# Two small loads moved in the weight queue of a recurrent loop, and eight more weight blocks loaded ahead of it

## The chip, the cores and the metric

The kernel runs on one core of a Trainium2 chip. The metric is device time in microseconds (us). Every run named here was put in the fast state by its own time, but for one repeat of one experiment, which is left out. Single executions of one kernel scatter by some 0.5%, and a profiled execution is one of the timed ones. So sizes are taken from the timed ratios, and traces are used to say where the time lies. The record marks every run as correct. One of them (e14) was made wrong on purpose, and the check passed it all the same, so the check does not guard what that run broke.

## The reference, cut to what matters

Two heads are computed and concatenated. Head B, a state-space convolution, comes first in the kernel and concerns us only in that the weights of head A are preloaded during its last phase. Head A is the loop:

```python
for s in range(n_seg):                                # 64 segments of 32 rows
    xs = x[:, s * seg_len:(s + 1) * seg_len, :].copy()
    h = jnp.concatenate([mem, xs], axis=1)            # 8 memory rows + 32 rows
    q, k, v = (jnp.einsum('btd,dhe->bhte', h, W) for W in (Wq, Wk, Wv))   # 32 heads of 128
    scores = jnp.einsum('bhqe,bhke->bhqk', q, k) * scale      # then mask, softmax p
    o = jnp.einsum('bhqk,bhke->bhqe', p, v)
    o = jnp.einsum('bhte,hed->btd', o, Wo)
    mem = o[:, :M, :].copy()                          # the next segment needs this one
    outs.append(o[:, M:, :])
```

(The three projections are written as one line here.) The steps can't overlap much, since each needs the memory rows of the one before. The kernel keeps only a part of the four weights (32 MB) on the core and loads the rest again in every step.

## The kernel before

A step uses 64 weight blocks of 512 KB. Most are resident, two are kept packed in PSUM, and 17 are streamed in each step through a ring of five slots. All streamed blocks are issued by the sync engine, in program order, so one queue carries the weights and the small loads and stores between them. `between` hangs a small load ahead of a streamed block. The loop's matmuls work on the 8 memory rows and 24 of a segment's 32 rows (the "x columns"); keys, queries and values of the other 8 rows (the "left rows") were computed before the loop and are loaded. A block's slot is free when the last matmul on the block five loads earlier has ended.

```python
STREAM = {("k", 0): (0, 5), ("q", 0): (1, 5), ("k", 1): (0, 3), ("q", 1): (0, 4), ("v", 0): (0, 4), ("v", 1): (0, 4)}
STREAM_O = (0, 4, 8, 11, 13)
SLOTS = 5
EARLY = 26                                            # resident blocks loaded before the loop

def unit(key):                                        # cut: resident and kept blocks return at once
    between.pop(key, lambda: None)()                  # a small load first, on the same queue
    t_ = wst.tile([128, 2048], BF16, name="wst", tag="w%d" % (loads[0] % SLOTS))
    loads[0] += 1
    nc.sync.dma_start(out=t_[:], in_=WD[key][:])
    return t_

def load_pk(j):                                       # "left rows": 128 x 768, 192 KB
    pk = pers.tile([128, 768], BF16, name="pk", tag="pk")     # one buffer
    nc.sync.dma_start(out=pk[:], in_=PKd[j])
    return pk

def load_xt(j):                                       # "x columns": 128 x 192, 48 KB
    xt = work.tile([128, KC, XM], BF16, name="xt", tag="F")   # shares its buffer with lb0b
    nc.sync.dma_start(out=xt[:].rearrange("p k r -> p (k r)"), in_=XTd[j])
    return xt

for s in range(NS):
    between["k", 0, 5] = lambda: pks.append(load_pk(s))
    if s:
        between["k", 1, 3] = lambda: stores(s - 1, ob)
    a = quads("k", 0, range(KC))                      # key projection, half 0
    pk = pks[0]
    k0 = evac(a, "A")
    KT0 = new_kt(0)                                   # copies left keys out of pk
    a = quads("q", 0, range(KC))
    # ... cut: k 1, q 1, scores, softmax, v 0, v 1; lb0b (tag "F") is written
    pv0 = pv_x(0, V0, pb0, [lb0a, lb0b])              # first value product: last reader of lb0b
    # ... cut
    oproj(pp[:, 1, :], range(0, 7), o0)
    # ... cut: second value product
    oproj(pp[:, 1, :], (7,), o0)
    pv_l(pl_, 1, V1, L1)                              # second left product: last reader of pk
    if s + 1 < NS:
        between["o", 11] = lambda: put_xt(load_xt(s + 1))
    oproj(pp[:, 1, :], range(8, 12), o1)
    fetch(("o", 15))                                  # unpacks a kept block
    oproj(pp[:, 1, :], range(12, 16), o1)
    # ... cut: output cast, memory rows into hT
```

## Time and profile before

2635.57 us median of 3 runs (2634.26 to 2643.28). The prediction shows the profile's lines; this table has the marks that the later sections use, in us from the start of the span of the profiled execution.

| mark | before |
|---|---|
| last matmul of head B's inverses ends | 868.0 |
| first x columns issued on the sync queue | 870.1 |
| first output cast of the loop (end of step 0) | 925.4 |
| last output cast | 2572.3 |
| end of span | 2634.1 |

63 steps lie between the two casts. What is to be read from the table is that the loop is 1647 of 2634 us, so a microsecond a step is 2.4% of the kernel.

### The profile page before, as it was taken

To read this page: it belongs to the slowest core of one execution; us is meant where nothing else is said; L and a number is where in the kernel's file an instruction comes from. 1 tells how busy PE (TensorE), PEld (TensorE's weight loads), DVE (VectorE), ACT (ScalarE), POOL (GpSimd) and SP (SyncE) were. 2 spreads that over 40 slices of the span, in tenths; PEclk is the share of its full clock that TensorE was granted. 3 is DMA by queue.
4 is the path that set the end of the run, shared out by engine and by line. 5 is a ranking of instruction groups with operands and counts; after the bars stand their busy time and mean duration, and the time that the engine had idled before them with its cause. 6 is when DMAs were issued, how large, how long until landed. Compare 5 with 4: busy or idle time off the path is not lost.

```text
span 2634.1 us, 76564 instructions
## 1 busy us (share of the span) xinstructions
PE 2085.4 (79%) x32902; PEld 1106.9 (42%) x32902; DVE 1496.4 (57%) x3224; ACT 1023.4 (39%) x1550; POOL 312.6 (12%) x601
## 2 busy tenths in 40 slices
PE   1588788776887688888888888888888787888788
PEld 1364555532333244444444444444444444444444
DVE  9677787879882245454545454454545454545450
ACT  6888888931222123232323323232323232322221
POOL 2233333450001100000000000000000000000010
PEclk6799999988898799899999999999999999999999
DMA  5665864742338999999999999999999999999992
GB/s 138 163 193 172 243 177 138 191 133 80 119 131 296 340 362 356 351 360 363 355 357 356 373 350 367 351 367 358 362 359 356 361 361 359 354 370 354 358 366 88
DMA packets 382386, 763.17 MB, mean 290 GB/s; under 512 B 118678, under 2 KB 210806, under 8 KB 379998
## 3 DMA queue, kind: packets, MB, share of 16 engines
q1 hardware_dynamic: 364158, 704.64, 76.1%
q0 software_dynamic: 14128, 39.99, 4.5%
q10 hardware_dynamic: 3760, 13.65, 1.4%
q8 instruction: 257, 4.21, 0.6%
q14 instruction: 83, 0.68, 0.1%
HBM read 703.35 MB, written 67.88 MB: 293 GB/s over the span
## 4 chain that ended last, share of the span: by engine, by line
DMA 35%; PE 30%; DVE 14%; ACT 9%; issue 8%; SPq 1%; POOL 1%; ACTq 0%; DVEq 0%; POOLq 0%
PE acc L329 15%; DMA wst<-WD_k 13%; DMA wst<-WD_o 13%; DMA wst<-WD_q 4%; DMA wst<-WD_v 2%; PE pp L428 2%; PE pe L551 2%; ACT sn L1019 2%; PE tr L340 2%; PE pro L151 2%; ACT kM L994 1%; ACT E L991 1%; ACT ev L335 1%; DVE piece L268 1%; PE ups L850 1%
## 5 line engine op out<-in xcount | busy, mean ns | idle before, releaser
L329 PEld LDWEIGHTS <-hT 128*32 128x32 bf16 x12352 | 334.8, 99 | 502.0 <-issue 293.2
L329 PE MATMUL acc<-wst,hT 128*32 128x512 bf16 x3072 | 321.7, 403 | 164.3 <-DMA wst<-WD_k 91.9
L335 ACT CAST ev<-acc 128x512 bf16<-128x512 f32 x384 | 225.1, 586 | 455.7 <-PE acc L329 451.4
L428 PEld LDWEIGHTS <-oT 128*32 128x32 bf16 x8192 | 205.6, 97 | 160.8 <-issue 134.5
L329 PE MATMUL acc<-W_q,hT 128*32 128x512 bf16 x3072 | 235.0, 391 | 0.0
L329 PE MATMUL acc<-W_k,hT 128*32 128x512 bf16 x2816 | 222.2, 417 | 0.0
L428 PE MATMUL pp<-W_o,oT 128*32 128x256 bf16 x5120 | 213.6, 277 | 6.6 <-DMA W_o<-in_A_Wo_dram 6.6
L329 PE MATMUL acc<-W_v,hT 128*32 128x512 bf16 x3072 | 213.5, 381 | 6.3 <-DMA W_v<-in_A_Wv_dram 6.3
L268 DVE TENSOR_SCALAR piece<-keep 128x256 int32<-128x256 int32 (+1 forms) x640 | 189.2, 362 | 48.3 <-PE pp L428 31.4
L341 DVE COPY KT<-tr 128x512 bf16<-128x512 bf16 x64 | 27.2, 425 | 304.7 <-PE tr L340 304.7
L367 DVE TENSOR_REDUCE mx<-sc 128x8 f32<-128x320 f32 x128 | 62.4, 488 | 236.6 <-PE sc L360 236.4
L428 PE MATMUL pp<-wst,oT 128*32 128x256 bf16 x2560 | 130.3, 280 | 78.5 <-DMA wst<-WD_o 69.3
L348 POOL COPY KT<-pk 128x128 bf16<-128x128 bf16 x128 | 37.9, 296 | 958.9 <-PE acc L329 545.2
L1158 PE MATMUL yp<-Bt,mi 128*128 128x512 bf16 x384 | 115.1, 408 | 40.5 <-DMA mi<-MId 31.8
L341 ACT COPY QT<-tr 128x512 bf16<-128x512 bf16 x128 | 75.0, 586 | 179.2 <-PE tr L340 178.3
L415 ACT CAST oT<-pv 128x512 bf16<-128x512 f32 x128 | 75.1, 586 | 173.4 <-PE pv L401 171.7
L995 DVE SCALAR_TENSOR_TENSOR nr<-kM,ptt 128x656 f32<-128x656 f32 x128 | 104.9, 833 | 43.7 <-ACT kM L994 43.4
L151 PE MATMUL pro<-xTl,wsl 128*128 128x512 bf16 x512 | 117.8, 384 | 11.6 <-DVE kst L155 7.4
L369 ACT ACTIVATE sc<-sc 128x320 f32<-128x320 f32 x128 | 54.0, 422 | 153.0 <-DVE sc L368 150.3
L518 ACT CAST ob<-pp 128x128 bf16<-128x128 f32 x64 | 17.0, 266 | 246.2 <-DVE ob L517 246.2
L1074 PE MATMUL hps<-KT,MF 128*128 128x512 bf16 x384 | 94.4, 395 | 19.4 <-DVE x L1087 15.2
L994 ACT ACTIVATE kM<-ptt,magic 128x656 f32<-128x656 f32 x128 | 104.2, 814 | 6.8 <-PE ptt L931 6.8
(285 smaller groups left out, 3661.3 us busy)
## 6 DMA issues: line engine op xcount, KB each, us to landing
wst<-WD_o SPq DMA_DIRECT2D x320, 512.0 KB
wst<-WD_k SPq DMA_DIRECT2D x256, 512.0 KB
wst<-WD_q SPq DMA_DIRECT2D x256, 512.0 KB
wst<-WD_v SPq DMA_DIRECT2D x256, 512.0 KB
Ud<-ux POOLq DMA_DIRECT2D x16, 1024.0 KB, 4.7
uq<-Ud SPq DMA_DIRECT2D x32, 512.0 KB
pk<-PKd SPq DMA_DIRECT2D x64, 192.0 KB
wsl<-in_A_Wk_dram SPq DMA_DIRECT2D x16, 512.0 KB
```

Of the source, the lines that this page charges most:

```text
L151: nc.tensor.matmul(a[:], lhsT=w[:, kc, 128 * j:128 * j + 128], rhs=xTl[:, kc, :, :].rearrange("p s k -> p (s k)"), start=(kc == 0), stop=( ...
L268: nc.vector.tensor_scalar(out=out.bitcast(I32), in0=in_.bitcast(I32), scalar1=0, scalar2=None, op0=ALU.bitwise_or)
L329: nc.tensor.matmul(a[32 * g:32 * g + 32, o_:o_ + rhs.shape[1]], lhsT=hT[:, kc, :], rhs=rhs, start=(kc == 0), stop=(kc == KC - 1), tile_pos ...
L335: nc.scalar.copy(out=q[:], in_=a[:])
L341: eng(out=dst, in_=p[:, i, :, :, :])
L367: nc.vector.tensor_reduce(out=mx[:], in_=sc, axis=AX.X, op=ALU.max)
L415: nc.scalar.copy(out=o[:], in_=p[:].rearrange("p a (g q) -> p a g q", g=4))
L428: nc.tensor.matmul(po[32 * qt:32 * qt + 32, :], lhsT=oT[:, h % 4, (h % 16) // 4, :], rhs=columns(w, 1024 * hh + 256 * qt, 256)[0][1], star ...
L994: sc.activation(out=kM[:], in_=ptv, func=ACT.Identity, bias=magic[:])
L995: v.scalar_tensor_tensor(out=nrs[e // 4][:, e % 4].rearrange("p f t j -> p f (t j)"), in0=kM[:], scalar=MAGIC, in1=ptv, op0=ALU.subtract, ...
L1074: pe.matmul(ps[:], lhsT=MF[:, 4 * rr + mc, cs, 128 * kc:128 * kc + 128], rhs=rhs, start=(i == 0 and mc == 0), stop=(i == 1 and mc == 3))
L1158: pe.matmul(yp[:], lhsT=m_[:, cs, kc, :], rhs=Bt[:, kc, half, j, c_, :], start=(n == 0), stop=(n == 15))
```

## The change

Its intent: each small load is to stand in the queue where it need not wait longer than the block behind it would wait anyway. The x columns go from ahead of output block 11 to ahead of 13, the left rows from ahead of key block (0,5) to ahead of query block (0,1). And eight more resident blocks are loaded during head B's last phase (10 into buffers that were free by then, 24 as before), so that fewer are left for the first step.

```diff
-EARLY = 26
+EARLY = 24
...
-        between["k", 0, 5] = lambda: pks.append(load_pk(s))
+        between["q", 0, 1] = lambda: pks.append(load_pk(s))
         if s:
             between["k", 1, 3] = lambda: stores(s - 1, ob)
         a = quads("k", 0, range(KC))
+        k0 = evac(a, "A")
+        a = quads("q", 0, range(KC))
         pk = pks[0]
...
-        k0 = evac(a, "A")
         KT0 = new_kt(0)
-        a = quads("q", 0, range(KC))
         q0 = evac(a, "B")
...
-            between["o", 11] = lambda: put_xt(load_xt(s + 1))
-        oproj(pp[:, 1, :], range(8, 12), o1)
+            between["o", 13] = lambda: put_xt(load_xt(s + 1))
+        oproj(pp[:, 1, :], range(8, 14), o1)
         fetch(("o", 15))
-        oproj(pp[:, 1, :], range(12, 16), o1)
+        oproj(pp[:, 1, :], range(14, 16), o1)
...
     def residents():
+        def put(t_):
+            load_resident(tc, None, src, rest.pop(0), W_res, tc.nc.scalar, t_)
+        four = ahead.pool.tile([128, 4, 2048], BF16, name="W4", tag="kst")
+        for i in range(4):
+            put(four[:, i, :])
+        yield
+        two = ahead.pool.tile([128, 2, 2048], BF16, name="W2", tag="xTl")
+        for i in range(2):
+            put(two[:, i, :])
+            yield
+        for _ in range(4):
+            put(ahead.pool.tile([128, 2048], BF16, name="W1", tag="wsl", bufs=4))
+            yield
```

Cut: the pools are opened earlier and closed later so that these buffers exist, and the first four blocks are issued at the start of the second pointwise half.

More of the change, by code (lines that the diff above doesn't have):

```diff
@@ L175, with load_resident @@
     pass
-EARLY = 26
-def load_resident(tc, pool, src, key, W_res, eng=None):
-    t_ = pool.tile([128, 2048], BF16, name="W_%s" % "_".join(str(i) for i in key))
+EARLY = 24
+def load_resident(tc, pool, src, key, W_res, eng=None, t_=None):
+    if t_ is None:
+        t_ = pool.tile([128, 2048], BF16, name="W_%s" % "_".join(str(i) for i in key))
     (eng or tc.nc.sync).dma_start(out=t_[:].rearrange("e (h d) -> e h d", h=2) if key[0] == "o" else t_[:], in_=src(key))
@@ L600, in part_b @@
     v.memset(magic[:], MAGIC)
+    ahead.open(ahead.ctx)
     ctx_m = ctx.enter_context(ExitStack())
@@ L603, in part_b @@
     MF = mfp.tile([128, 16, 2, 512], BF16, name="MF")
-    ctx_p = ctx.enter_context(ExitStack())
-    ahead.open(ctx_p)
     ctx1 = ctx.enter_context(ExitStack())
@@ L1042, in part_b @@
     ctx1.close()
-    bp = ctx.enter_context(tc.tile_pool(name="b_B", bufs=2))
+    bp = ctx.enter_context(tc.tile_pool(name="b_B", bufs=1))
     Dsk = const.tile([128, D], BF16, name="Dsk")
@@ L1051, in part_b @@
     ktp = ctx2.enter_context(tc.tile_pool(name="b_KT", bufs=1))
+    bp0 = ctx2.enter_context(tc.tile_pool(name="b_B0", bufs=1))
     pw = ctx2.enter_context(tc.tile_pool(name="b_pw", bufs=1))
@@ L1171, in part_b @@
     for dh in range(2):
-        Bt = bp.tile([128, 4, 2, 2, 2, DH], BF16, name="Bt", tag="B")
+        Bt = (bp0, bp)[dh].tile([128, 4, 2, 2, 2, DH], BF16, name="Bt", tag="B")
         Bs.append(Bt)
         if dh == 1:
+            resident = residents()
+            next(resident)
             todo = [(0, c) for c in range(16)] + [(1, c) for c in range(16)]
@@ L1183, in part_b @@
     ctx2.close()
-    ctx_p.close()
     ctx_m.close()
-    resident = residents()
     for c in range(16):
@@ L1224 @@
     rest = Keys(RESIDENT)
-    rest.ctx = ctx_w
+    rest.ctx = ahead.ctx = ctx_w
     def residents():
+        def put(t_):
[11 more added lines that the diff above has]
+            yield
         pool = ctx_w.enter_context(tc.tile_pool(name="a_wre0", bufs=1, side="right"))
```

## The prediction

> **What bounds the kernel now.** I read the page first, then busy time by stage, then the waits of the DMA queue and of TensorE, then one iteration of the loop on the queue.
>
> The page's slices show three regimes: preparation with DMA at 2 to 8 tenths, a loop from about 870 us with DMA at 9, a short tail. The chain that ended last is mostly DMA of streamed weight blocks (`wst`).
>
> ```profile
> PE   1588788776887688888888888888888787888788
> ...
> DMA  5665864742338999999999999999999999999992
> ...
> DMA 35%; PE 30%; DVE 14%; ACT 9%; issue 8%; SPq 1%; POOL 1%; ACTq 0%; DVEq 0%; POOLq 0%
> ```
>
> Busy time by stage (us of PE, PEld, DVE, ACT, POOL, then granted clock, DMA share, GB/s). I cut at the start of the inverse phase that preloads weights, at its end, at the first output cast of the loop (925.4) and at the last (2572.3).
>
> ```profile
> 798.00:860.00 62.00, 49.95 (x205) 20.70 (x204) 12.15 (x31) 15.33 (x23) 8.13 (x15) 0.92 0.96 335
> 860.00:872.00 12.00, 8.32 (x45) 3.52 (x42) 3.87 (x10) 2.94 (x5) 5.22 (x25) 1.00 0.39 131
> 872.00:925.40 53.40, 32.03 (x424) 13.28 (x424) 13.40 (x36) 8.39 (x14) 1.25 (x4) 0.63 1.02 389
> 925.40:2572.30 1646.90, 1360.28 (x26839) 702.65 (x26840) 816.88 (x2268) 487.06 (x945) 70.79 (x203) 0.96 0.98 359
> ```
>
> The loop's 63 later steps take 1646.9 / 63 = 26.14 us each, at DMA share 0.98 and 359 GB/s. PE is busy 83%. The first step takes 53 us because it also loads 19 resident blocks. Between 860 and 872 the DMA is mostly idle.
>
> Waits of the DMA queue in the loop, then of PE (us in total, times, longest):
>
> ```profile
> SPq L298 <- PE pv L401: 163.7, 62, 3.1
> SPq L293 <- PE pp L401: 137.1, 62, 2.9
> ```
>
> ```profile
> PE acc L329 <- DMA wst<-WD_k: 85.4, 105, 2.0
> PE pp L428 <- DMA wst<-WD_o: 66.6, 80, 2.8
> PE acc L329 <- DMA wst<-WD_q: 29.8, 90, 1.6
> ```
>
> L298 loads the next x columns, L293 the left rows. Each blocks the queue for a reason that has nothing to do with the weights: 2.6 and 2.2 us per step. PE waits for streamed blocks 85.4 + 66.6 + 29.8 + 4.8 (values) = 187 us in the loop, 3.0 us per step. One step on the queue (start, duration), and the DMA in 4 us stretches of it:
>
> ```profile
> 1719.28 2.95 SPq L246 DMA_DIRECT2D wst<-WD_o  x3
> 1724.91 0.32 SPq L298 DMA_DIRECT2D xt<-XTd  x1
> 1725.29 1.76 SPq L246 DMA_DIRECT2D wst<-WD_o  x2
> 1727.13 0.38 SPq L246 DMA_DIRECT2D wst<-WD_k  x1
> 1729.48 0.32 SPq L293 DMA_DIRECT2D pk<-PKd  x1
> 1729.85 0.42 SPq L246 DMA_DIRECT2D wst<-WD_k  x1
> ```
>
> ```profile
> 1718.00:1722.00 4.00, 4.00 (x90) 2.02 (x76) 2.90 (x7) 2.15 (x5) 0.30 (x1) 1.00 0.94 351
> 1722.00:1726.00 4.00, 3.81 (x88) 1.61 (x80) 3.65 (x11) 1.87 (x5) 0.00 (x0) 1.00 0.99 380
> 1726.00:1730.00 4.00, 3.50 (x92) 2.48 (x94) 3.31 (x10) 1.10 (x2) 0.35 (x1) 1.00 0.75 243
> ```
>
> No issue goes out between 1722.2 and 1724.9; the two output blocks then follow the x columns back to back, so their slots had been free. One DMA latency later the share falls to 0.75. The loop is DMA-bound, but its queue is fed with two holes.
>
> **What the Trainium skill says.** "Perfetto Trace Analysis", section "Sequencer Loop" and its DMA timeline under "Per-instruction lifecycle": a DMA's semaphore wait is served in the issuing sequencer, before the window shown. So a waiting small load holds everything behind it. The trace agrees (the 2.7 us hole above). "DMA: Bandwidth & Descriptors", section "Issuing engines are not separate DMA queues": DMAs of the scalar and sync engines run on the same 16 engines. It agrees: with both issuing in 798 to 860 the share is 0.96, no more. So preloading gains only where those engines idle. "Perfetto Trace Analysis", section "Roofline": 358 GB/s is the per-core share, about 435 GB/s the ceiling of the 16 engines when one core is active. The loop's 359 with 389 in its first step says that the loop isn't at the ceiling.
>
> **The change part by part.** The streamed blocks (17 of 512 KB a step), the five slots and the arithmetic stay. Comparing the instruction orders, PE, VectorE and GpSimd keep the order of their work; what moves is the queue of the sync engine and the preloads issued by ScalarE.
>
> (a) x columns ahead of output block 13. Their buffer is free once the first value product of the step has been read, which PE reaches just before value block (1,4). The slot of output block 11 is freed by value block (1,0), earlier; that of 13 by (1,4), later. So the old place blocks 11 and the new one blocks nothing. I paired each streamed load with the last matmul on the block five loads before. Block 11 is issued a median 1.63 us after its slot is free, 13 is 0.63 us late; unhindered ones are 0.03 to 0.05 us late.
>
> (b) Left rows ahead of query block 1. Their buffer is read until the second left product, after output block 7. The slot of key block 5 is freed by output block 4, before it, that of query block 1 by output block 8, after it. Key block 5 is a median 2.56 us late, query block 1 0.39 us.
>
> What these holes cost: I put the block packets of steps 3 to 60 in order of their start. From one block to the next takes 1.33 to 1.4 us where the queue is full (query to value blocks), 2.19 from output 11 to 13 and 2.36 from key 5 to query 1. The small loads take DMA time themselves, 0.20 us (x) and 0.66 us (left rows), from their packets' durations. Lost are 2.19 - 1.35 - 0.20 = 0.64 us and 2.36 - 1.35 - 0.66 = 0.35 us, together 1.0 us a step or 63 us in 63 steps. That is a ceiling for the removal of the holes. PE's waits at the blocks concerned average 0.17 (o11), 0.77 (o13), 0.55 (key 5) and 0.23 us (query 1), 1.7 us a step, so PE can take the gain. I count a bit over half, 0.55 us a step. The ring has only five slots, PE frees them unevenly, and blocks that now come early may find PE late. 63 x 0.55 = 35 us.
>
> (c) 34 blocks ahead instead of 26. Eight resident blocks leave the first step, which runs at 389 GB/s: 8 x 524,288 B / 389 GB/s = 10.8 us off it (the first step is DMA-bound at share 1.02). Where they go: four are issued at the start of the second pointwise half, near 645 us, where the DMA share is 0.2 to 0.3: free, 4 x 1.4 = 5.6 us into at least 10 us of idle. The two kept blocks move on the queue from 797.8 us to about 772 us, because they now wait for a matmul that ends at 770 and no longer for VectorE. The preload phase thus has 30 blocks where it had 26 + 2, two more: 2 x 1.35 = 2.7 us at its share of 0.96. Preloading now goes on to the last but one inverse, into the stretch 860 to 872 with share 0.39, which has 12 x 0.61 = 7 us to spare. I charge 1 us. Net 10 us.
>
> Sum: 35 + 10 = 45 us; 2635.6 - 45 = 2590 us.
>
> **Rivals.**
> The small loads become late themselves. The x columns are now behind block 11 in the ring; their copy to hT must precede the fetch of the kept output block 15, and the left rows are needed for the scores. For it: the fetch's five copies take 1.48 us and sit near the end of the step. Against it: the x columns still land ahead of block 13, PE uses 13 and 14 first, and the copy is 0.35 us; the left rows are used only after the whole second key projection, over 5 us later. If it held, the loop would gain nothing or lose 0.3 us a step: 2625 to 2645.
>
> The holes are hidden anyway. DMA share is already 0.98, and a block that starts late may only push back a wait that PE would have had at a later block. For it: DMA is the slower of the two, and the share counts packets that wait on one another. Then only part (c) is left: 2625. Against it: 243 GB/s in the dip is a real loss of bytes.
>
> The holes are the whole loss. Then 63 + 10 = 73 us: 2562. For it: PE's waits allow it. Against it: the slots.
>
> Preload slows the inverses. ScalarE issues the preloads in order between its own copies, and a full set of outstanding transfers would hold up the copy of an inverse. The phase would lengthen by the 2.7 us or more and (c) would be worth 5 us.
>
> **Range and chances.** 2590 us. The loop's part is 16 to 54 us for savings of 0.25 to 0.85 us a step, the start 6 to 12 us: 2570 to 2614, widened to 2564 to 2616. Two per cent is 53 us, which needs 43 us or 0.68 us a step from the loop: a little over one in three. Faster 0.34, within 2% 0.64, slower 0.02.
>
> **What would show it.** Right: the queue's waits at the x columns and left rows fall from 301 us to a small fraction; the dip to 0.75 after the x columns goes; steps near 25.6 us; PE's waits for output and key blocks fall by about 35 us; first step near 43 us; four preloads near 645 us. Wrong: waits of the same size that reappear at blocks 13 or query 1, or on GpSimd's copy to hT and the fetch of block 15; a step still near 26.1 us with the queue's waits gone (rival two); an inverse phase longer by over 3 us.

## The result, and the profile after

2554.9 us median of 4 runs (2542.52 to 2569.86), against 2639.43 us (2634.26 to 2646.12, 4 runs) for the kernel before. Ratio 0.9681, 95% interval 0.9613 to 0.9749: faster. A ratio here is the mean time of one kernel's fast runs over that of the other's of the same rounds, so not quite the ratio of the medians. The prediction was 2590 us, with 2616 to 2564 as its range: the result lies below it.

The page of the changed kernel, the DMA busy tenths in 40 slices and the chain that ended last:

```profile
DMA  5665756543346999999999999999999999999992
...
DMA 33%; PE 28%; DVE 17%; ACT 9%; issue 8%; SPq 1%; POOL 0%; ACTq 0%; DVEq 0%; POOLq 0%
```

The three regimes are the same, and the chain is still DMA first and PE second: the change did not hand the kernel to another engine. Busy time by stage (window, its length, busy us of PE, PEld, DVE, ACT, POOL, then granted clock, DMA share, GB/s), with the windows cut at the changed kernel's own marks:

```profile
802.50:872.00 69.50, 57.76 (x233) 24.02 (x236) 13.08 (x33) 17.78 (x28) 10.78 (x28) 0.91 0.92 322
872.00:877.00 5.00, 0.35 (x8) 0.29 (x8) 0.60 (x3) 0.59 (x1) 2.64 (x12) 0.91 0.52 203
877.00:921.90 44.90, 28.64 (x424) 12.43 (x424) 14.94 (x39) 8.31 (x14) 1.28 (x4) 0.69 0.97 364
921.90:2500.50 1578.60, 1330.32 (x26838) 694.97 (x26840) 818.64 (x2268) 486.97 (x945) 70.26 (x203) 0.98 1.00 375
```

The loop takes 1578.6 us where it took 1646.9, that is 25.06 us a step for 26.14; the DMA moves 375 GB/s for 359. Of the 71.6 us between the two profiled executions 68.3 lie in the loop. The first output cast comes 3.5 us earlier, although head B happened to run some 4 us late in this execution. The tail is equal (62.0 and 61.8).

Waits of the DMA queue in the loop (total us, times, longest). L247 is the streamed blocks, L294 the left rows, L299 the x columns, L310 one of the two stores:

```profile
SPq L247 <- PE acc L330: 416.1, 578, 2.7
...
SPq L294 <- PE pp L402: 101.8, 61, 2.2
...
SPq L310 <- ACT ob L526: 63.6, 63, 2.5
SPq L299 <- PE pv L402: 52.7, 62, 0.9
```

In the kernel before, where the streamed blocks are L246, the first of these lines was:

```profile
SPq L246 <- PE acc L329: 349.0, 507, 1.9
```

The two small loads wait 154.5 us in place of 300.8. The streamed blocks wait longer for slots that PE's matmuls hold, 522.8 us in place of 419.4 (the lines shown, and those for output blocks: 106.7 and 70.4). The left rows still wait 1.6 us a step, yet that wait now costs next to nothing: the slot of the block behind them comes free at about the same time. With each streamed load paired with the last matmul that used its slot, the median delay from "slot free" to "issued" is:

| block | before, us | after, us |
|---|---|---|
| key (0,5) | 2.56 | 0.05 |
| query (0,1) | 0.39 | 0.05 |
| output 11 | 1.63 | 0.04 |
| output 13 | 0.63 | 0.15 |

PE's waits for streamed blocks in the loop:

```profile
PE acc L330 <- DMA wst<-WD_k: 62.0, 72, 2.1
PE acc L330 <- DMA wst<-WD_q: 50.7, 104, 2.3
...
PE pp L429 <- DMA wst<-WD_o: 27.4, 46, 1.5
```

With 4.4 us for values that is 144.5 us where it was 187. Output and key blocks fell, query blocks rose. The same place of one step on the sync queue (start, duration, what, how many issues in a row), and the DMA in 4 us stretches there:

```profile
1707.54 4.85 SPq L247 DMA_DIRECT2D wst<-WD_o  x4
1713.30 0.32 SPq L299 DMA_DIRECT2D xt<-XTd  x1
1713.71 0.38 SPq L247 DMA_DIRECT2D wst<-WD_o  x1
1714.85 1.26 SPq L247 DMA_DIRECT2D wst<-WD_k  x2
1717.75 0.32 SPq L294 DMA_DIRECT2D pk<-PKd  x1
1718.30 0.97 SPq L247 DMA_DIRECT2D wst<-WD_q  x2
```

```profile
1708.00:1712.00 4.00, 3.76 (x85) 1.85 (x85) 3.55 (x9) 2.36 (x5) 0.00 (x0) 1.00 0.99 392
1712.00:1716.00 4.00, 4.00 (x99) 2.39 (x87) 3.54 (x10) 1.59 (x3) 0.00 (x0) 1.00 1.00 379
1716.00:1720.00 4.00, 3.33 (x86) 2.30 (x82) 2.66 (x9) 0.59 (x1) 0.35 (x1) 1.00 0.95 356
```

Four output blocks go out before the x columns instead of three, and only one follows them: nothing had piled up behind them. The last stretch, share 0.75 and 243 GB/s before, has 0.95 and 356.

### The profile page after: what moved, and what is told of

It is laid out like the page before. It is cut to its first block, busy times and chain, and to the rows that moved or that the text cites. A ratio compares the mean times of both kernels' runs of the same rounds, so it can differ in the third digit from the quotient of the medians.

```text
span 2562.5 us, 76703 instructions
## 1 busy us (share of the span) xinstructions
PE 2055.3 (80%) x32856; PEld 1101.7 (43%) x32902; DVE 1498.0 (58%) x3224; ACT 1023.9 (40%) x1550; POOL 311.6 (12%) x601
## 4 chain that ended last, share of the span: by engine, by line
DMA 33%; PE 28%; DVE 17%; ACT 9%; issue 8%; SPq 1%; POOL 0%; ACTq 0%; DVEq 0%; POOLq 0%
DMA wst<-WD_k 16%; PE acc L330 12%; DMA wst<-WD_o 10%; PE pp L429 3%; DMA wst<-WD_v 3%; PE pe L552 2%; ACT sn L1019 2%; PE pro L151 2%; PE tr L341 2%; ACT kM L994 1%; DVE piece L269 1%; PE ups L850 1%; ACT E L991 1%; PE pro L138 1%; ACT ev L336 1%
## 5 line engine op out<-in xcount | busy, mean ns | idle before, releaser
L330 PEld LDWEIGHTS <-hT 128*32 128x32 bf16 x12352 | 326.8, 97 | 474.1 <-issue 256.0
L330 PE MATMUL acc<-wst,hT 128*32 128x512 bf16 x3072 | 313.6, 393 | 163.3 <-DMA wst<-WD_k 67.4
L330 PE MATMUL acc<-W,hT 128*32 128x512 bf16 x2560 | 205.7, 392 | 0.0
L330 PE MATMUL acc<-W_q,hT 128*32 128x512 bf16 x1792 | 135.1, 383 | 0.0
L330 PE MATMUL acc<-W_k,hT 128*32 128x512 bf16 x1536 | 112.6, 401 | 0.0
L303 POOL COPY hT<-xt 128x192 bf16<-128x192 bf16 x64 | 22.2, 347 | 728.1 <-DMA xt<-XTd 442.0
```

Of the source, the lines that this page charges most:

```text
L330: nc.tensor.matmul(a[32 * g:32 * g + 32, o_:o_ + rhs.shape[1]], lhsT=hT[:, kc, :], rhs=rhs, start=(kc == 0), stop=(kc == KC - 1), tile_pos ...
```

## The experiments

Theory: both small loads held issues of blocks whose slots were free, and the whole of these holes comes back as time. Rivals: the loop's gain is something else that came with the change (the granted clock, PE's time, the preloads), or only one hole mattered. Each change in us below is the ratio's distance from 1 times the median of the kernel before in that call (2641.9 us of 27 runs in the first, 2645.0 of 13 in the second, 2645.4 of 9 in the third, 2643.9 of 12 in the last). Five rounds each. Diffs give the lines changed against the kernel named. By the author's account two more builds, a second buffer for the left rows and a ring of six slots, did not fit on the core and never ran; the record holds nothing of them.

### First call: the parts alone

**e1_loop_only**: the kernel before with both moves, without the preloads.

```diff
-        between["k", 0, 5] = lambda: pks.append(load_pk(s))
+        between["q", 0, 1] = lambda: pks.append(load_pk(s))     # with k0, quads("q", 0) moved as in the change
-            between["o", 11] = lambda: put_xt(load_xt(s + 1))
+            between["o", 13] = lambda: put_xt(load_xt(s + 1))   # with oproj's ranges as in the change
```

> Only the two moves in the loop, preloads as before. Theory 1 (the two holes in the queue are the whole gain of the loop): 62 to 70 us faster than before, ratio 0.974 to 0.977, queue waits at x columns and left rows as in the changed kernel. Theory 2 (the prediction's sizing was right and the surplus comes from elsewhere, the preloads or chance): 35 us faster, ratio 0.987.

2553.79 us (2544.85 to 2564.30, 6 runs), ratio 0.9672 (0.9648 to 0.9697): -87 us. Its loop, in the profiled execution (the fastest of the six):

```profile
928.90:2481.20 1552.30, 1316.77 (x26839) 691.45 (x26840) 817.20 (x2268) 486.97 (x945) 70.81 (x203) 0.99 1.01 382
```

At 382 GB/s the two moves alone carry nearly all of the change.

**e2_preload_only**: the change without the moves in the loop.

```diff
-        between["q", 0, 1] = lambda: pks.append(load_pk(s))
+        between["k", 0, 5] = lambda: pks.append(load_pk(s))
-            between["o", 13] = lambda: put_xt(load_xt(s + 1))
+            between["o", 11] = lambda: put_xt(load_xt(s + 1))
```

> Only the 34 preloaded blocks, loop as before. Theory 1: 7 to 11 us faster, ratio about 0.9965, the step still 26.1 us. Theory 2: 30 us or more faster, ratio 0.988 or below, because the preloads would carry the surplus.

2637.39 us (2624.07 to 2646.65, 22 runs), ratio 0.9984 (0.9971 to 0.9998): -4 us. Its first step, from the x issue to the first cast, takes 44.8 us for 55.3, so -10.5. But the x issue comes 6.4 us after the last inverse matmul instead of 2.1, and that matmul ends 1.0 us later: -10.5 + 4.3 + 1.0, some -5 us at the first cast. What holds the issue is one wait, the memory rows of step 0, in the full change the same. Waits of the queue from 780 to 930 us, first the kernel before, then the changed one:

```profile
SPq L298 <- DMA m<-in_A_mem_dram: 10.3, 1, 10.3
```

```profile
SPq L299 <- DMA m<-in_A_mem_dram: 13.7, 1, 13.7
SPq L273 <- PE yp L1159: 12.2, 1, 12.2
```

The memory rows (16 KB) are issued by ScalarE as soon as the last inverse matmul has ended, in the kernel before (868.0 us) and in the changed one (872.0 us). What differs is how long they take to land: in the changed kernel, whose last preload is issued at 868.8 us, 161 preload packets of 4 KB still end after the rows were issued; in the kernel before (857.3 us) none do. The second line of the changed kernel is the kept blocks, which wait for an inverse's matmul (more on it below).

**e3_x_only**: the kernel before with the x columns alone moved.

```diff
-            between["o", 11] = lambda: put_xt(load_xt(s + 1))
+            between["o", 13] = lambda: put_xt(load_xt(s + 1))
```

> Only the x columns moved. Theory 1 by the holes' sizes (0.64 of 0.99 us a step): 40 us faster, ratio 0.985; the dip after the x columns is gone, that after the left rows stays. Rival: the second hole takes over the wait that the first one gave up, then under 15 us.

2610.83 us (2598.82 to 2622.10, 6 runs), ratio 0.9887 (0.9857 to 0.9917): -30 us.

**e4_left_only**: the kernel before with the left rows alone moved.

```diff
-        between["k", 0, 5] = lambda: pks.append(load_pk(s))
+        between["q", 0, 1] = lambda: pks.append(load_pk(s))     # with k0, quads("q", 0) moved as in the change
```

> Only the left rows moved. Theory 1 by the holes' sizes (0.35 of 0.99 us a step): 22 us faster, ratio 0.992. Rival: the first hole hides it, then under 8 us, and the two moves together are worth more than their sum.

2596.54 us (2587.49 to 2610.47, 6 runs), ratio 0.9835 (0.9809 to 0.9862): -44 us. Both holes matter, and the left rows' is not the smaller one, though the prediction had it so. PE's waits in the two loops, first with the x columns moved, then with the left rows moved:

```profile
PE acc L329 <- DMA wst<-WD_k: 108.3, 126, 2.4
PE acc L329 <- DMA wst<-WD_q: 48.3, 107, 2.1
...
PE pp L428 <- DMA wst<-WD_o: 27.1, 43, 1.7
```

```profile
PE pp L428 <- DMA wst<-WD_o: 66.0, 79, 2.4
PE acc L329 <- DMA wst<-WD_k: 48.7, 69, 1.8
PE acc L329 <- DMA wst<-WD_q: 38.8, 77, 2.3
```

With the x columns moved the output blocks' waits fall from 66.6 to 27.1 us, but those at key blocks, just behind the hole that is still there, grow from 85.4 to 108.3. With the left rows moved key blocks fall to 48.7, and output blocks stay at 66.0. So part of what the first move wins is lost in the second hole, and the singles (30 + 44 = 74 us) are less than both together (87), by a difference at the edge of the noise (0.005 in the ratio, the intervals together give as much).

### Second call: other ways to the same end, and a wrong place

**e5_small_off_queue**: the kernel before, both small loads at their old places in the program, but issued by GpSimd.

```diff
-        nc.sync.dma_start(out=pk[:], in_=PKd[j])
+        nc.gpsimd.dma_start(out=pk[:], in_=PKd[j])
-        nc.sync.dma_start(out=xt[:].rearrange("p k r -> p (k r)"), in_=XTd[j])
+        nc.gpsimd.dma_start(out=xt[:].rearrange("p k r -> p (k r)"), in_=XTd[j])
```

> The kernel before with the x columns and the left rows in their old places of the program, but issued by GpSimd on its own queue. Theory 1 (what costs is that the weights' queue stands still behind a small load): as fast as the two moves, 80 to 95 us faster than before, ratio 0.965 to 0.970. Rival (it is the order in which the bytes reach the DMA engines, or the time of use, that matters): the bytes come at the same moments as before, so at most 20 us faster.

2577.93 us (2572.47 to 2582.25, 4 runs), ratio 0.9746 (0.9721 to 0.9770): -67 us. The places are the old ones and the queue alone is relieved, so it is the waiting in the weights' queue that cost the time. It is 20 us short of the moves; why is left open. The distances between blocks (explained below) show only where: those of key blocks (0,0), (1,0) and (1,3) are together some 0.8 to 0.9 us a step longer than before, (1,0) most.

**e8_x_earlier**: e4 with the x columns ahead of output block 8, still longer before their buffer comes free.

```diff
-            between["o", 11] = lambda: put_xt(load_xt(s + 1))
+            between["o", 8] = lambda: put_xt(load_xt(s + 1))
```

> The left-rows-only kernel with the x columns queued still earlier, ahead of output block 8: the hole in the queue is about 1 us a step longer. Theory 1: 40 to 65 us slower than the left-rows-only kernel (2597), so about 2650. Rival (holes of this size are mostly hidden by the five slots): within 15 us of it.

2669.51 us (2660.35 to 2673.88, 6 runs), ratio 1.0087 (1.0064 to 1.0111). Against e4 that is 0.0252 x 2645 = 67 us more, slightly beyond what was expected. The waits at the x columns and the loop's window:

```profile
SPq L298 <- PE pv L401: 250.1, 61, 5.5
```

```profile
922.80:2606.10 1683.30, 1408.68 (x26838) 726.08 (x26840) 816.95 (x2269) 486.68 (x945) 70.29 (x203) 0.92 0.94 352
```

One small load in a worse place: the wait grows from 163.7 to 250.1 us, the loop is longer than before although the other hole is closed, and the clock falls with it to 0.92.

**e6_stores_off_queue**: the changed kernel with the two stores of each step issued by GpSimd instead (they wait 63.6 and 35.1 us in the queue).

```diff
-        nc.sync.dma_start(out=OLd[s // 8]..., in_=ob[:, 1, :])
+        nc.gpsimd.dma_start(out=OLd[s // 8]..., in_=ob[:, 1, :])
-            nc.sync.dma_start(out=rows, in_=ob[:, 0, :])
+            nc.gpsimd.dma_start(out=rows, in_=ob[:, 0, :])
```

> The changed kernel with the two stores of a step issued by GpSimd instead of the sync engine, where they wait 69 + 35 us in all. Theory 1 extended (any wait of that queue costs): 15 to 35 us faster than the changed kernel, about 2530 us. Rival (a wait that ends before the queue runs dry costs nothing; the block after the stores is issued only 0.3 us after its slot is free): within 8 us of the changed kernel's 2554.

2667.53 us (2646.72 to 2697.07, 8 runs, the slowest in the slow state), ratio 1.0088 (1.0050 to 1.0126): 0.0407 x 2639 to 0.0453 x 2645, some 107 to 120 us slower than the changed kernel, and both expectations missed. One wait of ScalarE in the loop, absent in the changed kernel, says why:

```profile
ACT QT L342 <- DMA out_dram<-ob: 268.8, 63, 6.8
```

There the stores stand behind GpSimd's copy of the left keys and go out about 3 us later (a median 3.9 us after the output cast begins, where it was 0.95). They read `ob`, whose buffer the next step's QT takes over: the copy to QT waits for a store, and begins a median 1.8 us later in the step, 116 us in 63 steps. A queue was relieved, and a buffer was held.

**e7_pe_more**: the changed kernel with the mask's matmul (128 x 320) issued three times in place of once, which leaves the result as it is. By the spacing of matmuls in the trace that is an estimated 34 us more of PE work in the loop.

```diff
-            nc.tensor.matmul(sc[:], lhsT=ident[:], rhs=mask..., start=True, stop=False, ...)
+            for _ in range(3):
+                nc.tensor.matmul(sc[:], lhsT=ident[:], rhs=mask..., start=True, stop=False, ...)
```

> The changed kernel with the mask matmul of both scores done three times instead of once, same result: 4 matmuls of 320 columns a step, about 0.53 us of TensorE work, 34 us in the loop. If TensorE's own time sets the step after the change (theory 2: fewer half-clock stretches gave a good part of the gain): 30 us or more slower than the changed kernel. If the loop is still bound by the feed of blocks (theory 1): 5 to 20 us slower.

2569.07 us (2559.22 to 2584.16, 6 runs), ratio 0.9717 (0.9685 to 0.9749). Against the same kernel without it (e10 below) that is 0.0082 x 2645 = 22 us, against its first four runs 10. PE's time counts, but not in full, by about half (the intervals allow 12 to 31 us of the 34 against e10): the loop is bound neither by DMA alone nor by PE alone.

### Third call: the preloads, and two attempts to go on

**e10_after_again**: the changed kernel itself, to have it in this call.

```diff
 (no difference to the changed kernel)
```

> The changed kernel once more, unedited, beside the next two. If the preloads are worth the 10 us that their stage shows, and the loop is as in the loop-only kernel: ratio to before 0.9633 or so (0.9672 of the loop-only kernel less 0.4 points). If something in the loop gives the preloads' gain back, as the first four runs hint: 0.967 again.

2549.97 us (2544.73 to 2554.30, 4 runs), ratio 0.9635 (0.9616 to 0.9653), inside the first result's interval and four times narrower. It is -97 us; by its ratio the changed kernel is 0.0037 x 2642 = 10 us better than the moves alone (e1, another call; the intervals allow 2 to 18).

**e11_places_only**: the changed kernel with 26 blocks ahead in the new places.

```diff
-EARLY = 24
+EARLY = 16
```

> The changed kernel with its new places in memory and its earliest four preloads, but 26 blocks ahead as before: the other eight are loaded in the first step. If the first step's 11 us are a true gain of the eight blocks: 6 to 12 us slower than the changed kernel in the same call, first step near 56 us. If the loop gives them back: no difference in time.

2555.20 us (2553.37 to 2563.36, 4 runs), ratio 0.9661 (0.9642 to 0.9681): 7 us slower than e10, as expected, though at the edge of the noise (0.0026 in the ratio, with 0.0027 either way). Its first step is 55.0 us, as before the change.

**e9_mem0_sync**: the changed kernel with the memory rows of step 0 loaded by the sync engine, so that they stand behind no preload.

```diff
-        nc.scalar.dma_start(out=m0[:], in_=mem0)
+        nc.sync.dma_start(out=m0[:], in_=mem0)
```

> The changed kernel with the first memory rows (16 KB) loaded by the sync engine, not behind the last preloads on ScalarE's queue. In the trace the wait of the loop's first x columns for it falls from 4.8 us to about 2 us; time 2 to 4 us less than the changed kernel, which the timing may not resolve. Rival: the first block loads wait instead, no gain.

2549.48 us (2544.34 to 2550.74, 4 runs), ratio 0.9630 (0.9613 to 0.9647): no gain. The rows are issued at 870.9 us, again when the last inverse matmul has ended, and the x columns still come 4.6 us after it, with 155 preload packets ending after the rows' issue. So it is not the place in ScalarE's queue that delays them.

**e12_stores_at_end**: stores by GpSimd again, but called at the end of their own step, ahead of the copy that delayed them, and the memory rows by the sync engine.

```diff
-        if s:
-            between["k", 1, 3] = lambda: stores(s - 1, ob)
+        if s + 1 < NS:
+            stores(s, ob)                             # at the end of the step; dma_start by gpsimd in it
```

> The changed kernel with the two stores of a step issued by GpSimd right at the end of the step (not behind its copy of the left keys, as in the stores run that lost 113 us), and the memory rows loaded by the sync engine. If that loss came from the tile of the stores being held 4 us longer: the loss is gone, and 0 to 15 us are gained on the changed kernel (the queue's 104 us of waits at stores end before it runs dry). If software-issued stores are slow in themselves: still 50 us or more slower.

2565.26 us (2554.22 to 2568.39, 5 runs), ratio 0.9681 (0.9657 to 0.9706): 12 us slower than e10. The hold is gone:

```profile
ACT QT L342 <- DMA out_dram<-ob: 6.2, 2, 3.4
```

So the loss of over 100 us in e6 came from the late stores and not from GpSimd as such, all but about 12 us of it. What these 12 are was not looked into further. The stores are better left where they are.

### Last call: what was still open

Open were the size of the left rows' hole, and whether PE's time counts in the kernel before as it does after.

**e13_pe_more_before**: the edit of e7 in the kernel before.

```diff
-            nc.tensor.matmul(sc[:], lhsT=ident[:], rhs=mask..., start=True, stop=False, ...)
+            for _ in range(3):
+                nc.tensor.matmul(sc[:], lhsT=ident[:], rhs=mask..., start=True, stop=False, ...)
```

> The kernel before with the mask matmul of both scores done three times, same result: 0.53 us of TensorE work a step, 34 us in the loop, as in the run on the changed kernel, which lost 15 to 20. If the holes in the queue bind the loop before: 3 to 15 us slower than before, so the 30 us of TensorE time that the changed kernel has less in its loop can explain at most a third of that of its gain. If TensorE's time counts in full (half-clock stretches then explain 30 us of the gain): 25 us or more slower.

2664.19 us (2649.02 to 2669.18, 7 runs), ratio 1.0067 (1.0041 to 1.0093): +18 us of the estimated 34, between the two expectations. It is again about half (11 to 25 us), so there is no sign that the change made PE's time count more.

**e14_no_left_loads**: the changed kernel, left rows loaded in step 0 only. The result is wrong on purpose.

```diff
-        between["q", 0, 1] = lambda: pks.append(load_pk(s))
+        between["q", 0, 1] = lambda: pks.append(pk if s else load_pk(s))
```

> The changed kernel with the left rows loaded in the first step alone (wrong result on purpose): 63 loads of 192 KB fewer. If such a load takes 0.66 us of the DMA engines' time a step, as the prediction subtracted: 40 us faster than the changed kernel (2550), about 2510. If it takes the 0.2 us a step by which the distance of the blocks beside it grew where the load moved: 10 to 18 us faster, about 2536.

2539.52 us (2533.52 to 2542.85, 4 runs), ratio 0.9601 (0.9577 to 0.9626): 0.0034 x 2644 = 9 us faster than e10 (another call; 1 to 17), or some 0.15 us a step for the removal of the whole load, where the prediction had charged 0.66.

### The distances between blocks

To see where in a step the time went, the 128 packets of 4 KB of each block were put in order of their start, and the distance from the middle packet of one block to that of the next was averaged over the steps. Us a step, leading to the block named; e10 stands for the changed kernel:

| to block | before | x moved (e3) | left moved (e4) | changed (e10) | no left loads (e14) |
|---|---|---|---|---|---|
| key (0,5) | 2.24 | 2.40 | 1.42 | 1.38 | 1.39 |
| query (0,1) | 1.66 | 1.73 | 1.88 | 1.90 | 1.37 |
| output 11 | 2.13 | 1.38 | 2.11 | 1.39 | 1.38 |
| output 13 | 1.61 | 1.79 | 1.55 | 1.72 | 1.67 |
| key (1,0) to query (1,4), four | 5.77 | 5.74 | 5.90 | 5.77 | 6.23 |
| all 17 | 26.02 | 25.69 | 25.53 | 24.76 | 24.64 |

From before to changed, the x pair (outputs 11 and 13) falls from 3.74 to 3.11, by 0.63, the left pair (key (0,5), query (0,1)) from 3.90 to 3.28, by 0.62, and the other thirteen together by 0.01. That is 1.26 us a step, 79 us in 63 steps. The distances of a step add up to the step, so it is no second measurement that the two traces' loops differ by 79 us too (1646.9 above, and for e10):

```profile
920.60:2488.50 1567.90, 1327.46 (x26838) 695.31 (x26840) 818.61 (x2269) 486.26 (x945) 70.33 (x203) 0.99 1.00 378
```

Nor is one execution exact. By a second count of the packets, the two pairs fall by 1.3 us in all three executions that have both moves (e10, the one of the first result, e1), but the other thirteen are 0.2 us a step longer than before in that of the first result, whose loop is 68 us shorter, and 0.2 shorter in e1's. That is 13 us either way; the timing of e1, 87 us, is the measure of the whole. (The long distance is the one that leads to the block behind the small load; the prediction's 2.19 "from output 11 to 13" and 2.36 "from key 5 to query 1" are put one block too late: its lines of the queue show the gap ahead of output 11.) With x alone moved the left pair grows by 0.23: the queue stands longer at the remaining hole (155.0 us at the left rows for 137.1).

## Why the prediction was right or wrong

**The mechanism was right.** The two loads held issues of blocks whose slots were free; the moves alone (e1) give 87 us, the loads on another queue (e5) 67, and one load in a worse place (e8) costs 67, a part of it by the clock (below). The blocks named are the ones whose delays and distances fell, and the dip is gone.

**The x columns' hole came out right, partly by luck:** 0.64 us a step predicted, 0.63 by the distances. With the prediction's own 1.35 for an unhindered block the pair had 3.74 - 2.70 = 1.04 us too much before, and not 0.84, and keeps 3.11 - 2.70 = 0.41 after, where 0.20 was charged for the load. The hole and what stays of it were both taken too small, by the same 0.2 us. This is an estimate: no run took the x load away.

**The left rows' hole was mis-sized**, and this is the first term of the sum that failed: "2.36 - 1.35 - 0.66 = 0.35" was 0.62. Two things lie in it. The hole was read from one distance, while the one beside it was longer too: against a step without hole or load (e14: 1.39 + 1.37) the left pair of before has 3.90 - 2.76 = 1.14 us too much and not 1.01. And the load's own time was taken from its packets' durations as 0.66, while in the changed kernel, where the load stands in a full queue, it adds 3.28 - 2.76 = 0.52. The packets' durations depend on the place (their sum is 0.65 before, and 0.57 to 0.59 in the two executions of the changed kernel), and they aren't the time that a load takes from others; 192 KB at the loop's 378 GB/s are 0.52 us. 1.14 - 0.52 = 0.62. So the ceiling was 0.64 + 0.62 = 1.26 us a step or 79 us, not 63.

**"I count a bit over half" failed most.** The whole came. That the two pairs are 1.25 us shorter is the size of the holes over again; that it was kept is shown by the other thirteen distances, which gave nothing back (0.01 in e10, 0.2 either way in the two other executions), and by the timing of e1 (87 us). The reason that the prediction gave for the discount, blocks that come early and find PE late, is seen in the queue, whose waits for slots grew by 103 us (419.4 to 522.8); issue follows 0.04 to 0.15 us after the slot is free, so the slot is what it waits for. But the DMA engines stayed at work meanwhile (share 1.00, 0.98 before), so it cost nowhere near half. The step that failed is this charge. In us of the loop: 35 were predicted; the mis-sized hole adds 0.27 x 63 = 17, the discount 63 - 35 = 28, which makes 80, against 68 and 79 in the two profiled executions and 87 by the timing of e1. The discount was right about something else. When the load itself is taken away too (e14), its place in the queue gets 0.53 us shorter, but the four blocks from key (1,0) to query (1,4) get 0.46 longer, and about a quarter reaches the time. The queue's wait for the left rows (101.2 us) is then gone, and that for slots held by the output blocks' matmuls has grown by nearly as much (115.3 to 211.2). So the slots do bind, only after these two holes are gone.

**The preloads were about right:** 10 us predicted, 4 (e2), 7 (e11) and 10 (e1 against e10) measured, each with 4 to 8 us of noise either way. The first step fell by 10.2 us in the profiled pair (10.8 predicted; to 45.1 us from the x issue, where "near 43", counted from 872 us, stands for 44.5 from that mark), and the four early preloads came at 648 us. The inverses were not slowed: from the first to the last inverse matmul 198.9 us before and 198.6 after. What the prediction did not see is the memory rows, which land later while the last preloads are still under way and take back 2.8 us (x columns 4.9 for 2.1 us after the last inverse); e9 shows that issuing them on the other engine doesn't win it. And the kept blocks did not move to 772 us but to 788: they wait 12.2 us for a matmul of the inverses, the second line shown under e2.

**The signs it named.** PE's waits for output and key blocks fell by 62.6 us (35 named), those for query blocks rose by 20.9; together with the values they fell by 42. Queue waits were to fall "to a small fraction" and only halved: it is not the wait that costs, but the part of it in which the next slot is already free.

**Of the rivals**, "the holes are the whole loss" (2562) came nearest, and even it was too small by the mis-sized hole. "The holes are hidden anyway" fell with e1; "the small loads become late" with the trace of the changed kernel, where PE waits 2.6 us in the whole loop for hT and 1.5 us for the unpacked pieces; "preload slows the inverses" with the 198.6 us above.

**What stays open** is a second term, the granted clock. The clock records show 118 us at half clock in the loop before, 60 and 46 in the two executions of the changed kernel, 30 in e1's; PE's busy time in the loop falls with it from 1360 to 1330 us. The prediction left this out. By e7 and e13 about half of PE's time counts, so by this estimate some 15 us of the gain may have come by this way, and some 26 of e8's 67 us (277 us at half clock, PE busy 1408.7 us for e4's 1357.3). It is not the cause of the rest: e4 has 125 us at half clock, and in that same execution its loop is still 30 us shorter (1617.0). How much it is was not settled, nor whether the fewer stalls raised the clock, nor were the 20 us by which e5 falls short.

The best version is the changed kernel itself; e9 equals it, and no other correct one beat it.

## What to carry to other kernels

A small load in a queue of large ones belongs where its own buffer comes free no later than the slot of the block behind it; the test is the delay from "slot free" to "issued" of the blocks behind, not the length of the small load's wait. When a hole is sized, add up all distances around it against a place without one, and for what the load itself costs take its bytes at the queue's rate (0.52 us here, as measured) rather than the sum of its packets' durations (0.66). If there is no measured reason for a discount on a ceiling, the ceiling itself belongs inside the range.

## What the Trainium skill lacked or had wrong

- "Perfetto Trace Analysis", section "What "DMA-bound" means": it lists three bounds: particular DMA engines, the issuing sequencer solid with DMA slices, and SBUF reads. It lacks a fourth, seen here: one queue that is held by a small load waiting for its own buffer, while slots for large loads behind it are free. The loop's DMA share was 0.98 with it and 1.00 to 1.01 without, so the share hardly shows it; the two moves took 3.3% off the kernel (e1).
- "Perfetto Trace Analysis", section "DMA Optimizations": it suggests that inputs and outputs be issued by different engines. Here that was slower both times, by over 100 us where the stores then stood behind a waiting copy (e6: 268.8 us of waits for their buffer) and by 12 us where they did not (e12, which also loads the memory rows by another engine; e9 with that alone lost nothing). The page doesn't say that a late store holds the buffer that it reads.
- "TensorE: Matmul & The Clock Gate", section "HAM oscillation — how this bites in real kernels": it gives as the rule no gaps of PE over about 3.4 us. In the loop before no gap was longer than 2.85 us, and yet the clock records have 28 stretches at half clock, 118 us. So the rule is not enough; the page's own next section allows for many shorter gaps, without a number, and the runs here don't give one either.
- No page says what a small load adds to a queue that large ones keep full. A 192 KB load between 512 KB blocks took 0.52 us of its place, which is its bytes at the loop's 378 GB/s, and some 0.15 us a step of the kernel's time (e14), where the sum of its packets' durations was 0.66 in the prediction.
